# Residual sums two items further on, a row store ahead of other stores, and one load moved into the y products

## Chip, cores and metric

The kernel runs on one core of a Trainium2 chip. The metric is the time of one execution on the device, in microseconds. Engines are named as the profile names them: PE (TensorE), DVE (VectorE), ACT (ScalarE), POOL (GpSimd), SP (SyncE, which issues the DMAs here).

## The reference, cut to what matters

```python
x = A_x                                      # 1 x 2048 x 512, float32
for _ in range(2):                           # two layers
    n = layernorm(x)
    a, b = n @ dft_hid_re.T, n @ dft_hid_im.T
    x = x + (dft_seq_re @ a - dft_seq_im @ b)        # Fourier mixing over the sequence
    n = layernorm(x)
    h = gelu(layernorm(n) @ w1)                      # then shifted by +1, -1, +2, -2 rows
    x1 = n + shifted(h) @ w2
    x = x + x1 + gelu(layernorm(x1) @ w3) @ w4
```

The change touches the Fourier mixing: its residual sum, the sums over rows that the next layernorm needs, and the order of the work beside it.

## The kernel before

All products run in a split form: a float32 operand is cast to a high part (fp32r) and a low part (what is left of it), and each product is three matmuls, high by high, high by low, low by high (`mm3`, line 294). Matrices come through *items*. An item is a block of 128 x 1024 words that is loaded raw by SP (`issue_dma`, line 208), turned into its high part (`stage_one`) and its low part (`stage_two`), and used by TensorE as the moving operand.

- A *plain* item: ScalarE casts the raw block (L241), VectorE subtracts to get the low part (L258).
- A *one* item (half as wide): VectorE first takes a difference of the two halves of a raw block (L243), ScalarE casts it (L244), VectorE makes the low part (L258).
- A *by1* or *by0* item: VectorE takes a difference of two raw blocks (L247), ScalarE casts it (L248), VectorE makes the low part (L258).

Parts lie in a ring of four places. `stream()` hands item i to TensorE; as it does so it issues stage one of item i + 3 (whose place is that of item i - 1, so this waits until TensorE is through with i - 1) and stage two of item i + 2. Each engine takes its instructions in the order in which the program issues them.

The mixing of a layer runs over four chunks (c = 0 to 3) of 512 output rows. A chunk has two phases.

**x products** (`x_phase`): for k = 0 to 7 a plain and a one item, here called x0 to x15; x(2k) feeds PSUM banks PC and PB, twelve matmuls, x(2k+1) feeds PA, six. From chunk 1 on, the eight items of the hidden DFT for the chunk before stand between them (h0 to h7, twelve matmuls each, into PD): h3 in front of x8, h4 and h5 in front of x10, h6 and h7 in front of x12. h0 to h3 give the first half of the chunk's rows, h4 to h7 the second half. When a half is complete, `add_y` adds PD to the residual rows: two SCALAR_TENSOR_TENSOR of VectorE (L596), each with the sum over the row. The first half's rows stand in X0 (tmp rows 0 and 1), the second half's in X1 (tmp rows 4 and 5). After the last x item, ScalarE copies PC, PB (L518, L520) and later PA (L526) to SBUF.

**y products** (`y_phase`): for k = 0 to 7 a by1 item (PC, then PD) and a by0 item (PB, then PA), here called y0 to y15, twelve matmuls each. The first matmul of y0 writes PC again.

Around each x item i stand three things, in this order: `stream()`, `run_late(i)` (small work that was put off to this item) and `hook(i)`. `late[9]` holds the squares of the first half's rows and `late[10]` their statistics; the second half's are done in the y phase. The hook of layer 0 also prepares weights for later stages: sums of weight blocks (`sum_at`: load, make, low part and keep, each at an item's number) and splits of weight blocks (`W_REST`: load, high, low part with its store). In chunks 1 and 2 a third weight sum uses tmp rows 0 to 3 (`sum_t`): its load stands at 11, its three adds (L492) and cast (L1646) at 13, its low part (L1650) at 14, its store at 18. `W_REST` uses tmp rows 2 and 3. Both therefore wait for earlier stores from tmp.

The hook loads the residual rows into X1 at 4 and X0 at 5, and stores X0's finished rows to x1d at 9. In chunk 3 it also brings back rows of x1d (`BACK`): rows 0 and 1 at item 8, 2 and 3 at 11, 4 and 5 at 13 (units of 128 rows). These rows are normed in the stage behind the y products; 4 and 5 during the second of its four hidden products.

All DMAs stand in SP's one queue, and an issue that has to wait for a tile holds up those behind it.

## Time and profile before

| | us |
|---|---|
| median of 3 runs | 1419.0 (1418.55 to 1420.17) |
| the profiled execution | 1418.97 |
| its span, first to last instruction | 1417.2 |
| PE busy | 1409.0 |
| VectorE busy | 1191.3 |
| ScalarE busy | 765.5 |

The granted TensorE clock was 1.000 over the whole span. A timeline row has the start in us, the duration in us, the engine, the line, the operation and the names of what it writes and reads; `x2` means that two neighbours were merged, and a bracket gives the idle time of the engine before it and what ended that. Instructions of one engine overlap at their ends: the distance from start to start is what one costs in a row of several. A row of the view of waits has the total wait in us, how often it occurred, and the longest. An SPq row is the issue of a DMA, not its transfer.

### The profile page before, as it was taken

The page shows a single profiled execution, that of the slowest core. Times are in us where ns is not written, and L with a number is a line of the kernel's source. Part 1 is how long each engine was busy: PE and PEld are TensorE (multiplying, and loading weights), DVE is VectorE, ACT ScalarE, POOL GpSimd, SP SyncE. Part 2 cuts the span into 40 slices and gives each one's busy share as a digit, 9 for nine tenths or more (in the row PEclk, how much of TensorE's full clock was granted, in tenths as well). Part 3 has the DMA queues.
Part 4 walks back from the last instruction along what each step waited for, and adds up shares of the span by engine and source line. Part 5 has one row for each costly group of instructions (what it writes and reads, how often), then busy time and mean ns, then how long its engine had stood idle before and what let it go on. Part 6 is the DMA issues. An engine that isn't in the chain of part 4 may idle for free.

```text
span 1417.2 us, 18479 instructions
## 1 busy us (share of the span) xinstructions
PE 1409.0 (99%) x6669; PEld 1181.8 (83%) x6669; DVE 1191.3 (84%) x1684; ACT 765.5 (54%) x1072; POOL 68.2 (5%) x105
## 2 busy tenths in 40 slices
PE   9999999999999999999999999999999999999998
PEld 8888788888788888988888888888888888899887
DVE  7988998998988789956789979879889788897776
ACT  6664555556566655534555545645555566454351
POOL 2100000000001100000000000000000020000000
PEclk9999999999999999999999999999999999999999
DMA  8978858778774748865556476565587457687864
GB/s 290 306 236 302 268 194 274 241 230 309 255 228 146 253 165 264 257 247 180 195 177 218 136 225 206 166 220 170 193 265 237 134 141 245 188 250 252 297 205 160
DMA packets 158907, 316.18 MB, mean 223 GB/s; under 512 B 10848, under 2 KB 78816, under 8 KB 156896
## 3 DMA queue, kind: packets, MB, share of 16 engines
q1 hardware_dynamic: 158816, 315.01, 67.9%
q8 instruction: 52, 0.85, 0.2%
q14 instruction: 39, 0.32, 0.1%
HBM read 260.70 MB, written 54.26 MB: 222 GB/s over the span
## 4 chain that ended last, share of the span: by engine, by line
PE 94%; DVE 3%; DMA 1%; ACT 1%; issue 1%; SPq 0%; POOL 0%; DVEq 0%; ACTq 0%; POOLq 0%
PE psd L295 10%; PE psd L296 10%; PE psd L297 10%; PE psa L295 8%; PE psa L297 8%; PE psa L296 8%; PE psb L296 7%; PE psb L297 7%; PE psb L295 7%; PE psc L295 6%; PE psc L296 6%; PE psc L297 6%; DMA raw<-in_ws 1%; DVE ring L258 1%; DVE rest L492 0%
## 5 line engine op out<-in xcount | busy, mean ns | idle before, releaser
L241 ACT CAST ring<-raw 128x1024 fp32r<-128x1024 f32 x127 | 132.9, 1052 | 69.4 <-PE psd L297 30.6
L258 DVE TENSOR_TENSOR ring<-raw,ring 128x1024 fp32r<-128x1024 f32 x126 | 153.4, 1220 | 14.3 <-ACT ring L241 14.3
L295 PE MATMUL psd<-ring,rr 128*128 128x512 f32 x208 | 80.9, 389 | 0.0
L296 PE MATMUL psd<-ring,rr 128*128 128x512 f32 x208 | 80.9, 389 | 0.0
L297 PE MATMUL psd<-ring,rr 128*128 128x512 f32 x208 | 80.9, 389 | 0.0
L248 ACT CAST ring<-ring0f 128x1024 fp32r<-128x1024 f32 x28 | 29.5, 1054 | 46.9 <-DVE ring0f L247 46.9
L258 DVE TENSOR_TENSOR ring<-ring1f,ring 128x512 fp32r<-128x512 f32 (+1 forms) x56 | 53.3, 952 | 0.8 <-ACT ring L244 0.7
L346 POOL TENSOR_TENSOR rows<-ve,mhalf 128x4 f32<-128x4 f32 x16 | 18.2, 1136 | 735.2 <-DVE ve L345 735.2
L295 PE MATMUL psc<-ring,ay 128*128 128x512 f32 x128 | 50.0, 391 | 1.6 <-ACT rr11f L518 1.6
L296 PE MATMUL psb<-ring,ay 128*128 128x512 f32 x128 | 50.0, 391 | 1.2 <-DVE ring L258 1.2
L297 PE MATMUL psb<-ring,ay 128*128 128x512 f32 x128 | 49.8, 389 | 0.0
L295 PE MATMUL psb<-ring,ay 128*128 128x512 f32 x128 | 49.8, 389 | 0.0
L296 PE MATMUL psc<-ring,ay 128*128 128x512 f32 x128 | 49.8, 389 | 0.0
L297 PE MATMUL psc<-ring,ay 128*128 128x512 f32 x128 | 49.8, 389 | 0.0
L297 PE MATMUL psa<-ring,ay 128*128 128x512 f32 x126 | 49.0, 389 | 0.0
L295 PE MATMUL psa<-ring,ay 128*128 128x512 f32 x126 | 49.0, 389 | 0.0
L295 PE MATMUL psd<-ring,ay 128*128 128x512 f32 x126 | 49.0, 389 | 0.0
L296 PE MATMUL psd<-ring,ay 128*128 128x512 f32 x126 | 49.0, 389 | 0.0
L296 PE MATMUL psa<-ring,ay 128*128 128x512 f32 x126 | 49.0, 389 | 0.0
L297 PE MATMUL psd<-ring,ay 128*128 128x512 f32 x126 | 49.0, 389 | 0.0
L314 POOL TENSOR_TENSOR rs<-ve,mhalf 128x2 f32<-128x2 f32 (+2 forms) x33 | 28.5, 863 | 412.4 <-DVE nb L313 393.4
L697 DVE TENSOR_TENSOR rg<-gt,rg 128x512 fp32r<-128x512 f32 x32 | 22.1, 690 | 29.6 <-ACT rg L696 29.6
(834 smaller groups left out, 4617.1 us busy)
## 6 DMA issues: line engine op xcount, KB each, us to landing
raw<-in_ws SPq DMA_DIRECT2D x183, 512.0 KB, 5.4
raw<-in_hs SPq DMA_DIRECT2D x56, 512.0 KB, 3.7
w3b<-w3d SPq DMA_DIRECT2D x11, 1792.0 KB, 8.5
w4r<-w4d SPq DMA_DIRECT2D x22, 512.0 KB, 3.5
un<-w4s SPq DMA_DIRECT2D x40, 256.0 KB, 3.7
un<-w4d SPq DMA_DIRECT2D x38, 256.0 KB, 4.4
x1d<-tmp SPq DMA_DIRECT2D x12, 512.0 KB, 6.8
xs<-x1d SPq DMA_DIRECT2D x12, 512.0 KB, 5.2
```

What stands on the lines that cost most here:

```text
L241: nc.scalar.copy(dest[:, a:b, 0], r[0][:, a:b])
L248: nc.scalar.copy(dest[:, :, 0], lo)
L258: nc.vector.tensor_tensor(lo, src, hi.bitcast(F32), op=ALU.subtract)
L295: nc.tensor.matmul(o, lh, rh, start=first, stop=False, skip_group_check=more)
L296: nc.tensor.matmul(o, lh, rl, start=False, stop=False, skip_group_check=more)
L297: nc.tensor.matmul(o, ll, rh, start=False, stop=last, skip_group_check=more)
L314: nc.gpsimd.tensor_tensor(rs[:, :n], ve[:, :n], mhalf[:, 0, :n], op=ALU.pow)
L346: nc.gpsimd.tensor_tensor(rs, ve, mhalf[:, :, :2], op=ALU.pow)
L697: nc.vector.tensor_tensor(lo, src, hi.bitcast(F32), op=ALU.subtract)
```

## The change

Four edits:

1. `add_y` is no longer called right behind the hidden product. The first half's stands in `late[8]` (behind `stream()` of x8), the second half's in `late[13]` (behind `stream()` of x13). This holds for chunks 1 to 3 of both layers. The squares and statistics stay where they were.
2. The third weight sum is made at 12 and its low part at 13, in place of 13 and 14 (chunks 1 and 2 of layer 0).
3. In the hook, the row loads at 4 and 5 and the row store at 9 are issued in front of the weight work of the same item (layer 0).
4. Rows 4 and 5 are brought back at y's k = 5 in place of item 13 (chunk 3 of both layers).

```diff
-BACK = {8: 0, 11: 2, 13: 4}
+BACK = {8: 0, 11: 2}
...
                 if h % 4 == 3:
-                    at_mix = c == NC - 1 and h > 4
-                    add_y(c - 1, h // 4, PD, X1 if h > 4 else X0, 2 * k + 1 if h < 4 else "y", "10" if at_mix else 2 * k + 2 if h < 4 else "y+")
+                    if h < 4:
+                        args = (c - 1, 0, PD, X0, 2 * k + 1, 2 * k + 2)
+                    else:
+                        args = (c - 1, 1, PD, X1, "y", "10" if c == NC - 1 else "y+")
+                    late.setdefault(2 * k + h // 4, []).append(lambda args=args: add_y(*args))
                 h += 1
...
         if c < 3:
-            sum_at(c, *units[2], sum_t, 11, 13, 14, 18)
+            sum_at(c, *units[2], sum_t, 11, 12, 13, 18)
...
-                if layer == 0:
-                    prepare_at(c, i)
-                    for f, n in W_REST.get((c, i), ()):
-                        f(n)
                 j = (c - 1) * TC
                 if i == 4:
                     rows(X1, xin, j + 2, 2, True)
                 if i == 5:
                     rows(X0, xin, j, 2, True)
                 if i == 9:
                     rows(X0, x1d, j, 2, False)
+                if layer == 0:
+                    prepare_at(c, i)
+                    for f, n in W_REST.get((c, i), ()):
+                        f(n)
...
+                if c == NC - 1 and k == 5:
+                    rows(xs[2], x1d, 4, 2, True)
```

## The prediction

> **What bounds the kernel now.** I read the page's busy shares first, then who TensorE waits for, then the timeline of TensorE around each of those waits.

> ```profile
> PE 1409.0 (99%) x6669; PEld 1181.8 (83%) x6669; DVE 1191.3 (84%) x1684; ACT 765.5 (54%) x1072; POOL 68.2 (5%) x105
> ...
> PE psc L295 <- ACT rr11f L518: 1.6, 2, 0.8
> PE psb L296 <- DVE ring L258: 1.2, 1, 1.2
> ...
> 148.16 0.39 PE L297 MATMUL psa<-ring,ax 128*128 128x512 f32 x1
> 149.31 0.50 PE L295 MATMUL psc<-ring,ay 128*128 128x512 f32 x1 [0.76 <-ACT rr11f L518]
> 149.65 0.40 PE L296 MATMUL psc<-ring,ay 128*128 128x512 f32 x1
> ...
> 354.73 0.39 PE L295 MATMUL psb<-ring,ay 128*128 128x512 f32 x1
> 356.27 0.50 PE L296 MATMUL psb<-ring,ay 128*128 128x512 f32 x1 [1.15 <-DVE ring L258]
> ...
> 361.62 0.39 PE L295 MATMUL psb<-ring,ay 128*128 128x512 f32 x1
> 362.07 0.50 PE L296 MATMUL psb<-ring,ay 128*128 128x512 f32 x1
> ```

> TensorE is busy 99% of 1417.2 us, so every microsecond that it waits shows in the time. Matmuls start 0.23 us apart where nothing is late (851.48 to 851.71 in a fence below); a longer step is a stall. Three places matter here. In chunk 1 of layer 0 the first y matmul starts 1.15 after the last x matmul, and the next step is 0.34 instead of 0.23: **1.03** lost. Chunk 2 has its twin (the wait is listed twice): about **1.1**. In chunk 3 the steps at 354.73 and 361.62 are 1.54 and 0.45: 1.31 and 0.22 too long, with 0.11 behind each: **1.76**. So 3.9 us is all that the change could take away.

> **What an x chunk's end hangs on.** VectorE and ScalarE of chunk 1, from the end of the last hidden product (h7) on:

> ```profile
> 139.75 0.69 DVE L596 SCALAR_TENSOR_TENSOR tmp<-psd,tmp 128x512 f32<-128x512 f32 x1 [2.17 <-PE psd L297]
> 140.43 0.69 DVE L596 SCALAR_TENSOR_TENSOR tmp<-psd,tmp 128x512 f32<-128x512 f32 x1
> 141.05 0.69 DVE L243 TENSOR_TENSOR ring3f<-raw 128x512 f32<-128x512 f32 x1
> 141.65 1.22 DVE L258 TENSOR_TENSOR ring<-raw,ring 128x1024 fp32r<-128x1024 f32 x1
> 143.15 1.23 DVE L247 TENSOR_TENSOR ring0f<-raw,raw 128x1024 f32<-128x1024 f32 x1 [0.28 <-PE psb L297]
> 144.29 0.68 DVE L258 TENSOR_TENSOR ring<-ring3f,ring 128x512 fp32r<-128x512 f32 x1
> 144.90 1.60 DVE L492 TENSOR_TENSOR tmp<-tmp 128x512 f32<-128x512 f32 x3
> 146.42 1.22 DVE L247 TENSOR_TENSOR ring1f<-raw,raw 128x1024 f32<-128x1024 f32 x1
> 148.69 1.22 DVE L1650 TENSOR_TENSOR tmp<-tmp 128x1024 fp32r<-128x1024 f32 x1
> ...
> 147.72 1.05 ACT L248 CAST ring<-ring1f 128x1024 fp32r<-128x1024 f32 x1
> 148.68 1.07 ACT L518 COPY rr11f<-psc 128x512 f32<-128x512 f32 x2
> ```

> In order: the two residual sums; x15's difference and x14's low part; y0's difference (ring0) and x15's low part; the three weight sums; y1's difference (ring1); later the weights' low part (L1650). ScalarE casts y1's high part as soon as its difference is there, then empties PC (two copies of 0.53), and the first y matmul writes PC. So **the start of the y products follows y1's difference**: 146.42 + 1.30 to the cast, 0.96 to the copy, 0.58 for its first half, 0.05 to TensorE, 149.31. Whatever stands ahead of y1's difference on VectorE counts in full once this chain is late.

> **The change, part by part.** *Second residual sums, behind x15's low part.* x15's difference writes the ring place of h7, so it can't start before h7 ends (140.41) wherever the sums stand. Before, the first sum ran in that wait for nothing and only the second cost 0.62. After, both stand in a stretch with no idle time ahead of y1's difference: 1.30 (139.75 to 141.05).

> Chunk 1, layer 0, with the weight sums at 12 and their low part at 13, from 140.43: 0.60 (x15's difference, 141.05 to 141.65) + 1.14 (x14's low part; what is 1024 wide steps by 1.14, as 143.15 to 144.29) = 142.17; weight sums 1.52 (144.90 to 146.42) = 143.69, past the 143.13 for which y0's difference waited, so that 0.28 of idle is used; 1.14 + 0.61 = 145.44; residual sums 1.30 = 146.74; the weights' low part, which stood behind y1's difference and now stands ahead of it, 1.14 = 147.88. y1's difference moves from 146.42 to 147.88: **+1.4 to 1.5** on a stall that is already there. (The weight load must be in by 142.17 for this. Here the row store was the last that it waited for, so it goes out sooner and I take it to be in time; it was in by 144.90, so 2.7 more is the utmost.)

> Chunks without weight sums have some slack (chunk 1 of layer 1; its chunks 2 and 3 look the same; then chunk 3 of layer 0):

> ```profile
> 848.22 1.22 DVE L247 TENSOR_TENSOR ring1f<-raw,raw 128x1024 f32<-128x1024 f32 x1
> 849.52 1.05 ACT L248 CAST ring<-ring1f 128x1024 fp32r<-128x1024 f32 x1 [0.68 <-DVE ring1f L247]
> 850.49 1.06 ACT L518 COPY rr11f<-psc 128x512 f32<-128x512 f32 x2
> 851.48 0.39 PE L297 MATMUL psa<-ring,ax 128*128 128x512 f32 x1
> 851.71 0.39 PE L295 MATMUL psc<-ring,ay 128*128 128x512 f32 x1
> ...
> 345.68 1.06 ACT L518 COPY rr11f<-psc 128x512 f32<-128x512 f32 x2
> 346.57 0.39 PE L295 MATMUL psc<-ring,ay 128*128 128x512 f32 x1
> ```

> The first copy ends 850.49 + 0.58 + 0.05 = 851.12; TensorE wants it at 851.71: slack 0.59. Pushed by 1.30 (1.22 where neither sum waits), it is 0.63 to 0.71 late, and the slow step adds 0.11: **+0.8** in each of three chunks, 2.4. In chunk 3 of layer 0 the slack is 346.57 - 346.31 = 0.26: 1.04 + 0.11 = **+1.1**.

> *First residual sums, one item on, and chunk 2's loads.*

> ```profile
> 220.30 0.68 DVE L596 SCALAR_TENSOR_TENSOR tmp<-psd,tmp 128x512 f32<-128x512 f32 x1
> 221.94 1.22 DVE L258 TENSOR_TENSOR ring<-raw,ring 128x1024 fp32r<-128x1024 f32 x1 [0.34 <-ACT ring L241]
> ...
> SPq L1629 <- DMA x1d<-tmp: 2.7, 1, 2.7
> ...
> 228.87 1.35 SPq L1598 DMA_DIRECT2D w3d<-tmp  x2
> 230.26 0.82 SPq L206 DMA_DIRECT2D x1d<-tmp  x1
> ...
> 236.37 0.90 SPq L1629 DMA_DIRECT2D tmp<-in_w  x2
> ...
> DMA to landing us min/median/max: 6.4/6.5/6.6
> ...
> 240.80 1.23 DVE L258 TENSOR_TENSOR ring<-raw,ring 128x1024 fp32r<-128x1024 f32 x1
> ...
> 244.01 1.61 DVE L492 TENSOR_TENSOR tmp<-tmp 128x512 f32<-128x512 f32 x3
> ```

> In chunks 2 and 3 the first sums filled the time until ScalarE's cast of h4 was ready, for which its low part still waited 0.34. Behind that low part they push what follows by 1.2 to 1.3: h5's low part and the load that it frees, the stores behind that, and the loads behind the stores. TensorE itself isn't held: PD's first half is free at 221.94 + 1.14 + 0.69 = 223.8, and h4 needs it two items (eighteen matmuls, 4.08) after h3, which ended about when the first sum started, 220.30: some half us in hand. In chunk 1 and in layer 1 VectorE reached this place before h3 had ended, so the sums cost nothing there. Putting the row store first doesn't free chunk 2's weight load (L1629): it fills all four rows of tmp, and two of them are the source of the w3d stores (L1598), which are now last. The load landed at 236.84 + 6.6 = 243.4; I expect 243.4 to 244.7. The weight sums, one item earlier, want it at 240.80 + 1.14 = 241.94. This is **the new wait**: VectorE stands, with y0's difference, x15's low part (TensorE needs it, and will stall inside x15), the residual sums and y1's difference queued behind. From a landing of 244.3: weight sums 245.85, 1.75 to 247.6, residual sums 248.9, low part 250.0. y1's difference stood at 244.01 + 1.52 = 245.53, so chunk 2 costs **+4.3** (3.6 at 243.4, 4.8 at 244.7; 2.1 if the load is in time).

> [...] The change moves the wait earlier and, in chunk 2, the issue not at all. [...]

> In chunk 3 the weight load at 10 waits for a w3d store that now stands behind the row store, and y0's raw stands behind that load in SP's queue: between nothing and the 1.3 of the shift; I take 0.4.

> *Rows 4 and 5.*

> ```profile
> 344.14 1.43 SPq L206 DMA_DIRECT2D xs<-x1d  x1
> 353.86 1.23 DVE L247 TENSOR_TENSOR ring0f<-raw,raw 128x1024 f32<-128x1024 f32 x1 [1.57 <-DMA raw<-in_ws]
> ...
> xs<-x1d SPq DMA_DIRECT2D x12, 512.0 KB, 5.2
> ```

> In chunk 3 of layer 0 this load holds SP for 1.43 and moves 512 KB ahead of y's raw loads; VectorE then stands 1.57 for one of them, and the low part behind it is what TensorE waits for at 356.27. Gone, and with TensorE itself later by 1.1 or more, both stalls vanish: **-1.76**. At its new place (after ten y items of twelve matmuls, 2.72 each) it has six y items and a hidden product, some 21 us, until ScalarE norms the rows, against 5.2 to land: nothing; without that cover it would cost what of 5.2 is left. Layer 1 has no such stall: nothing. X0's and X1's loads ahead of other loads: they land before the sums that read them, which would wait for them otherwise: nothing.

> **Sum:** 1.4 + 4.3 + (1.1 + 0.4 - 1.76) + 2.4 = +7.8 or +7.9. The profiled run took 1418.97 (span 1417.2), the median is 1419.0: **1427**.

> **Rivals.** (1) *Chunk 2's load is in time*, because the queue empties faster with another order. For it: the issue at 236.37 hangs on stores that could be issued sooner. Against it: the same bytes go ahead. Chunk 2 costs 2.1, and the sum is +5.7: 1424.7. (2) *Faster*: at the end of the x products there is slack that I don't see, so that y1's difference may be 1.3 later for nothing. It decides at y1's cast: with 0.7 more slack layer 1 costs nothing, and if the weights' low part also fits, the three stalls go: -3.9, 1415.1. For it: VectorE idles 2.17 ahead of the old place of the sums. Against it: x15's difference can't use that time, and cast and copy follow without a gap. (3) *No change*: the work moves in TensorE's shadow, and only chunk 1 of layer 0, already late, loses its 1.4, and chunk 3's 1.76 pays for it: 1418.6. [...] The waits listed above speak against it. (4) *Much slower*: the late first sums push chunk 3's raw load as far as chunk 2's weight load, and y0 there costs 4.3 in place of 1.5: 1429.7, or more.

> **Chances.** Forecast 0.53, with its own range 1425.5 to 1429 (the bounds of chunks 2 and 3); rival 1 0.22; rival 2 0.09; rival 3 0.08; rival 4 0.08. The range 1422 to 1430 leaves out rivals 2 and 3 and half of 4. By 0.2%, 2.8 us (about what a measurement of this kernel can tell from no change): faster 0.09, same 0.08, slower 0.83.

> **What would show it.** Right: a wait of TensorE on L518 at all six ends of x products, about 0.7 in layer 1, over 2 in chunk 1 of layer 0 and more in chunk 2; VectorE idle before the weight sums in chunk 2, released by the load; no wait at chunk 3's y0 to y5 for a raw load. Wrong: layer 1's y products follow the x products without a gap, or y1's difference stands ahead of the residual sums.

## The result, and the profile after

| | before | after |
|---|---|---|
| median of 6 runs each, us | 1418.97 (1418.52 to 1420.57) | 1432.09 (1429.86 to 1433.05) |
| ratio after / before | | 1.0087 (1.0074 to 1.0100) |
| the profiled execution | 1418.97 | 1429.93 |
| its span | 1417.2 | 1428.0 |
| granted clock, mean over the span | 1.000 | 0.998 |

The change costs 13.1 us. The forecast was 1427, with a range to 1430: the side was right, the size 5.1 too small. The six runs of the kernel after are not alike: two took 1429.86 and 1429.93 at a mean granted clock of 0.998, four took 1431.94 to 1433.05 at 0.996. Before, the clock was 1.000.

The profile's page and its view of TensorE's waits, kernel after (columns of the second: who waited for what, us in total, times, longest):

```profile
PE 1411.7 (99%) x6669; PEld 1181.6 (83%) x6669; DVE 1190.6 (83%) x1684; ACT 764.5 (54%) x1072; POOL 67.4 (5%) x105
```

```profile
PE psc L295 <- ACT rr11f L521: 8.8, 6, 3.7
PE psa L296 <- DVE ring L258: 1.2, 1, 1.2
PE psb L296 <- DVE ring L258: 0.2, 1, 0.2
```

The copy of PC (L518 before, L521 now) is waited for six times in place of two: at the end of the x products of every chunk that has a residual sum. The wait on `psa` is the stall inside x15 in chunk 2 of layer 0. VectorE is as busy as before (1191.3 and 1190.6), and PE's busy time rose by 2.7 with the same 6669 instructions. Nothing was added; matmuls became slower. Where, the windows of that kernel show (columns: stretch in us and its length, busy us of PE, PEld, DVE, ACT, POOL with counts, **granted clock**, DMA share, GB/s). The stretches are 3.41 long and laid at the edges at which the clock changed:

```profile
148.58:151.99 3.41, 1.79 (x8) 1.49 (x9) 3.41 (x4) 3.37 (x6) 0.00 (x0) 1.00 0.63 195
151.99:155.40 3.41, 3.41 (x17) 2.83 (x16) 3.41 (x4) 2.49 (x4) 0.00 (x0) 1.00 0.61 189
247.56:250.97 3.41, 1.43 (x5) 0.86 (x5) 3.41 (x8) 1.23 (x2) 0.00 (x0) 1.00 0.21 85
250.97:254.38 3.41, 0.81 (x2) 0.72 (x3) 3.41 (x4) 2.39 (x5) 0.00 (x0) 0.50 0.40 117
254.38:257.79 3.41, 3.41 (x9) 2.63 (x9) 3.19 (x3) 3.41 (x6) 0.00 (x0) 0.50 0.66 207
257.79:261.20 3.41, 3.41 (x16) 2.80 (x16) 2.36 (x2) 1.11 (x2) 0.00 (x0) 1.00 0.80 296
```

Around the end of chunk 2's x products the clock is at half for two stretches, each behind one in which TensorE stood idle for long (1.98 and 2.60, which is 3.41 less its busy time; the stall inside x15 counts towards the first). In the second, TensorE is busy all the time and gets 9 matmuls through, in place of 16 or 17. A step there is 0.427, against 0.227 at full clock:

```profile
254.59 0.63 PE L297 MATMUL psc<-ring,ay 128*128 128x512 f32 x1
255.01 0.63 PE L295 MATMUL psc<-ring,ay 128*128 128x512 f32 x1
```

The long wait is thus paid twice, once as a wait and once as slow matmuls behind it. In chunk 1 (the first two rows of the windows) TensorE stood idle for 2.13 and the clock stayed at 1.00. (Two numbers for one stall are kept apart below: *idle* is the time in a timeline's bracket; *late* is what the step from the last matmul to this one has above 0.227, some 0.16 more. What a place *loses* is late, plus the 0.11 of the step behind it, plus slow matmuls.)

VectorE in chunk 2, kernel after:

```profile
241.05 1.23 DVE L258 TENSOR_TENSOR ring<-raw,ring 128x1024 fp32r<-128x1024 f32 x1
245.06 1.61 DVE L492 TENSOR_TENSOR tmp<-tmp 128x512 f32<-128x512 f32 x3 [2.79 <-DMA tmp<-in_w]
246.59 1.22 DVE L247 TENSOR_TENSOR ring0f<-raw,raw 128x1024 f32<-128x1024 f32 x1
247.72 0.69 DVE L258 TENSOR_TENSOR ring<-ring3f,ring 128x512 fp32r<-128x512 f32 x1
...
250.68 1.22 DVE L247 TENSOR_TENSOR ring1f<-raw,raw 128x1024 f32<-128x1024 f32 x1
```

This is the new wait, as forecast: VectorE stands 2.79 for the load of the weight rows; x15's low part comes at 247.72, too late for TensorE; y1's difference comes at 250.68, when TensorE had been through with x15 since 249.9; before, it came at 245.53, ahead of the last x matmul (247.21). And the end of an x phase of layer 1, TensorE:

```profile
859.38 0.39 PE L297 MATMUL psa<-ring,ax 128*128 128x512 f32 x1
860.23 0.50 PE L295 MATMUL psc<-ring,ay 128*128 128x512 f32 x1 [0.46 <-ACT rr11f L521]
860.57 0.39 PE L296 MATMUL psc<-ring,ay 128*128 128x512 f32 x1
```

A step of 0.85 and one of 0.34 where 0.23 each would do: 0.73, three times.

### The profile page after: what moved, and what is told of

Read it like the earlier page. It is cut to its first block, busy times and chain, and to the rows that moved or that the text cites. A ratio compares the mean times of both kernels' runs of the same rounds, so it can differ in the third digit from the quotient of the medians.

```text
span 1428.0 us, 18485 instructions
## 1 busy us (share of the span) xinstructions
PE 1411.7 (99%) x6669; PEld 1181.6 (83%) x6669; DVE 1190.6 (83%) x1684; ACT 764.5 (54%) x1072; POOL 67.4 (5%) x105
## 4 chain that ended last, share of the span: by engine, by line
PE 90%; DVE 5%; DMA 2%; ACT 2%; issue 1%; SPq 0%; DVEq 0%; POOL 0%; ACTq 0%
PE psd L295 9%; PE psd L296 9%; PE psd L297 9%; PE psa L295 8%; PE psa L297 8%; PE psa L296 8%; PE psc L295 6%; PE psb L296 6%; PE psb L295 6%; PE psb L297 6%; PE psc L296 6%; PE psc L297 6%; DVE ring L258 1%; DMA tmp<-in_w 1%; DVE ring0f L247 1%
## 5 line engine op out<-in xcount | busy, mean ns | idle before, releaser
L241 ACT CAST ring<-raw 128x1024 fp32r<-128x1024 f32 x127 | 132.6, 1051 | 68.6 <-PE psd L297 29.2
L258 DVE TENSOR_TENSOR ring<-raw,ring 128x1024 fp32r<-128x1024 f32 x126 | 153.6, 1220 | 18.5 <-ACT ring L241 18.2
L297 PE MATMUL psd<-ring,rr 128*128 128x512 f32 x208 | 80.9, 389 | 0.0
L296 PE MATMUL psd<-ring,rr 128*128 128x512 f32 x208 | 80.9, 389 | 0.0
L295 PE MATMUL psd<-ring,rr 128*128 128x512 f32 x208 | 80.9, 389 | 0.0
L295 PE MATMUL psc<-ring,ay 128*128 128x512 f32 x128 | 51.0, 399 | 8.8 <-ACT rr11f L521 8.8
L248 ACT CAST ring<-ring0f 128x1024 fp32r<-128x1024 f32 x28 | 29.5, 1054 | 46.3 <-DVE ring0f L247 46.0
L258 DVE TENSOR_TENSOR ring<-ring1f,ring 128x512 fp32r<-128x512 f32 (+1 forms) x56 | 53.3, 951 | 0.8 <-ACT ring L244 0.7
L248 ACT CAST ring<-ring1f 128x1024 fp32r<-128x1024 f32 x28 | 29.5, 1053 | 43.5 <-DVE ring1f L247 43.5
L296 PE MATMUL psc<-ring,ay 128*128 128x512 f32 x128 | 50.3, 393 | 0.0
L297 PE MATMUL psc<-ring,ay 128*128 128x512 f32 x128 | 50.3, 393 | 0.0
L296 PE MATMUL psb<-ring,ay 128*128 128x512 f32 x128 | 50.0, 391 | 0.2 <-DVE ring L258 0.2
L297 PE MATMUL psb<-ring,ay 128*128 128x512 f32 x128 | 49.8, 389 | 0.0
L295 PE MATMUL psb<-ring,ay 128*128 128x512 f32 x128 | 49.8, 389 | 0.0
L295 PE MATMUL psd<-ring,ay 128*128 128x512 f32 x126 | 49.4, 392 | 0.0
L297 PE MATMUL psd<-ring,ay 128*128 128x512 f32 x126 | 49.3, 391 | 0.0
L296 PE MATMUL psd<-ring,ay 128*128 128x512 f32 x126 | 49.3, 391 | 0.0
L297 PE MATMUL psa<-ring,ay 128*128 128x512 f32 x126 | 49.0, 389 | 0.0
L296 PE MATMUL psa<-ring,ay 128*128 128x512 f32 x126 | 49.0, 389 | 0.0
L295 PE MATMUL psa<-ring,ay 128*128 128x512 f32 x126 | 49.0, 389 | 0.0
## 6 DMA issues: line engine op xcount, KB each, us to landing
raw<-in_ws SPq DMA_DIRECT2D x183, 512.0 KB, 5.3
raw<-in_hs SPq DMA_DIRECT2D x56, 512.0 KB, 3.9
w4r<-w4d SPq DMA_DIRECT2D x22, 512.0 KB, 3.8
x1d<-tmp SPq DMA_DIRECT2D x12, 512.0 KB, 6.8
xs<-x1d SPq DMA_DIRECT2D x12, 512.0 KB, 5.7
```

What stands on the lines that cost most here:

```text
L241: nc.scalar.copy(dest[:, a:b, 0], r[0][:, a:b])
L248: nc.scalar.copy(dest[:, :, 0], lo)
L258: nc.vector.tensor_tensor(lo, src, hi.bitcast(F32), op=ALU.subtract)
L295: nc.tensor.matmul(o, lh, rh, start=first, stop=False, skip_group_check=more)
L296: nc.tensor.matmul(o, lh, rl, start=False, stop=False, skip_group_check=more)
L297: nc.tensor.matmul(o, ll, rh, start=False, stop=last, skip_group_check=more)
```

## The experiments

**Theory:** nearly everything that the change costs comes from what stands ahead of y1's difference on VectorE, and what the waits themselves don't explain comes from the granted clock, which falls behind a long wait. **Rivals:** the extra time has nothing to do with the wait's length (the moved stores and loads compete with others); or the queue is not it, and the loads alone set the x phases' ends. In all of them the instructions of one kernel keep their names, but line numbers move by a few.

| run | from | edit | median, us (low to high) | ratio to before (interval) |
|---|---|---|---|---|
| e1 | after | weight sums back to 13 and 14 | 1427.47 (1426.52 to 1428.97) | 1.0053 (1.0038 to 1.0068) |
| e2 | after | second sums at once | 1424.44 (1424.16 to 1425.94) | 1.0035 (1.0023 to 1.0048) |
| e4 | before | second sums alone put off | 1427.50 (1425.26 to 1428.36) | 1.0050 (1.0035 to 1.0065) |
| e5 | before | idle subtractions in layer 1 | 1432.54 (1431.45 to 1433.17) | 1.0087 (1.0072 to 1.0102) |
| e6 | after | first sums at once | 1430.40 (1427.89 to 1430.84) | 1.0070 (1.0056 to 1.0084) |
| e7 | after | row loads and store back | 1428.85 (1428.08 to 1430.50) | 1.0064 (1.0048 to 1.0079) |
| e3 | before | rows 4, 5 in the y products | 1418.71 (1417.78 to 1420.39) | 0.9995 (0.9986 to 1.0003) |
| e8 | before | e3, and weight sums at 14 and 17 | 1422.11 (1420.81 to 1424.64) | 1.0015 (1.0007 to 1.0024) |
| r1, r2 | after | none | 1431.41; 1433.13 | one run each |
| e10 | after | second sums at 14, weight sums at 18, 20 | 1417.40 (1416.33 to 1418.34) | 0.9986 (0.9977 to 0.9995) |
| e12 | before | e3, and weight sums at 18, 20 | 1416.76 (1415.33 to 1417.73) | 0.9979 (0.9970 to 0.9988) |

The kernel before had 1419.24 (beside e1, e2, e4, e5), 1419.29 (e3, e6, e7, e8) and 1419.46 (the rest).

### e1: the weight sums where they were

```diff
-            sum_at(c, *units[2], sum_t, 11, 12, 13, 18)
+            sum_at(c, *units[2], sum_t, 11, 13, 14, 18)
```

> The changed kernel with the third weight sum back at 13 and its low part at 14. Queue theory: the wait for chunk 2's weight load goes, since the sums stand behind the residual sums again (which end near 245.2, the load lands near 244.9). y1's difference then starts about 1.3 later than before the change in chunks 1 and 2, so the stalls there are about 2.3 us each; chunk 3 and layer 1 stay as in the changed kernel (+0.9, +2.2). Clock theory (the granted clock falls because TensorE waited 3.7 us in chunk 2): no wait above 2.5 us is left, the granted clock is 1.000 in every run, the time 1424 to 1425. Rival (the clock falls by itself, whatever TensorE waits): the clock stays at 0.996 to 0.998 and the time is 1426 to 1428.

Measured: chunk 2's stall inside x15 is gone, and y0 is 2.24 late in place of 3.85. That part of the forecast holds: the 2.79 for the load came from the earlier place. But the clock isn't 1.000. The windows of e1 in chunk 1:

```profile
148.11:151.52 3.41, 1.43 (x7) 0.88 (x6) 3.41 (x4) 3.27 (x6) 0.00 (x0) 1.00 0.41 131
151.52:154.93 3.41, 3.41 (x10) 2.63 (x9) 3.41 (x4) 2.74 (x6) 0.00 (x0) 0.50 0.48 179
```

An idle time of 1.98 was followed by a half-clock stretch in chunk 1, and chunk 2 shows the same; the chunks lost 3.85 and 3.95, of which 1.60 in each are slow matmuls. In the profile of the kernel after, 2.13 in chunk 1, which is longer, cost no clock. So the length of the wait alone doesn't decide; r1 and r2 below show what else does.

### e2, e6: one residual sum put back

```diff
-                    late.setdefault(2 * k + h // 4, []).append(lambda args=args: add_y(*args))
+                    if h < 4:
+                        late.setdefault(2 * k, []).append(lambda args=args: add_y(*args))
+                    else:
+                        add_y(*args)
```

> The changed kernel with the second half's residual sums back behind h7; the first half's stay late. Queue theory: the three waits of 0.6 us at the ends of layer 1's x products are gone (-2.2), chunk 1 of layer 0 stalls about 1.7 in place of 2.4, and chunk 2 still waits for its weight load inside x15 (1.3) and then some 2.6 in place of 3.85 at y0. Clock theory: the wait of 2.6 is too short to bring the clock down, or does so in some runs only; time 1424 to 1425 without, 2 to 3 more with it. Rival (the position of the second sums doesn't matter, the loads do): layer 1's waits stay and the time is 1430.

e6 is the mirror image (first sums at once, second put off):

> The changed kernel with the first half's residual sums back behind h3. Queue theory: VectorE no longer falls 1.3 us behind in chunks 2 and 3 of layer 0, the stores and loads behind h5's low part go out about 1.3 earlier, chunk 2's weight load lands near 243.6 in place of 244.9, and TensorE loses some 4 us there in place of 5.3 before the clock; chunk 3's y0 loses 1.1 in place of 1.9. Without the clock +6; with one to three half-clock windows of 3.4 us (each up to 1.7) 1426.5 to 1429.5. Rival (the store order alone makes the load late): chunk 2 stays as in the changed kernel, time 1431 to 1432.

The waits of TensorE in e2:

```profile
PE psc L295 <- ACT rr11f L524: 4.3, 3, 2.5
PE psa L296 <- DVE ring L258: 1.1, 1, 1.1
```

Three waits in place of six: with the second sums ahead of x15's difference again, layer 1 waits nowhere. This is the largest single part, and it is VectorE's queue and nothing else that was touched. One half-clock stretch is left, in chunk 2, where y0 is 2.63 late. In e6 VectorE stands 1.02 for chunk 2's weight rows in place of 2.79, so the put-off first sums had made that load later; there is no stall inside x15, y0 is 3.40 late in place of 3.85, and chunk 2 loses 5.12 in place of 7.37. In chunk 3 VectorE no longer waits for y0's raw load:

```profile
349.00 1.23 DVE L247 TENSOR_TENSOR ring0f<-raw,raw 128x1024 f32<-128x1024 f32 x1 [0.89 <-PE psb L297]
```

There y0 loses 1.07 in place of 1.89. Layer 1 keeps its three times 0.73. But in chunk 1 VectorE now stands 0.58 ahead of the weight sums (the trace names no releaser), y0 is 2.96 late, and the clock falls: 4.67 in place of 2.40. One place gives back most of what the others gained, so the median, 1430.40, lies above the expected 1429.5.

### e4: the second sums alone

```diff
+                    if h < 4:
+                        add_y(c - 1, 0, PD, X0, 2 * k + 1, 2 * k + 2)
+                    else:
+                        args = (c - 1, 1, PD, X1, "y", "10" if c == NC - 1 else "y+")
+                        late.setdefault(2 * k + 1, []).append(lambda args=args: add_y(*args))
```

> The kernel before with one edit: the second half's residual sums at item 13. Queue theory: layer 1 gets a wait of 0.62 us at each of three ends of x products (+2.2), chunks 1 and 2 of layer 0 get 1.2 to 1.3 more each, chunk 3 gets 1.1 and loses part of its 1.76 behind it since TensorE is later: 1424 to 1425.5, clock 1.000. Rival (VectorE's idle time ahead of the old place covers the sums): the time stays at 1419.

Five lines of the change, with every store, load and weight sum as before, cost 8.3 us. In the profile: chunk 1 loses 3.85 in place of 1.03, chunk 2 3.85 in place of 1.10, y0 of chunk 3 1.06, where it lost nothing, layer 1 three times 0.73. The expected 1424 to 1425.5 had the waits, but not the clock: it was to stay at 1.000. In chunk 1 TensorE was idle for 1.98 of one stretch (147.57 to 150.98, busy for 1.43 of 3.41), and the next was at half clock; chunk 2 lost as much, and the mean clock, 0.998, fits one such stretch in each. No transfer was moved here, so competition between transfers isn't needed for the clock's fall.

### e5: waits made on purpose

Two, three and four subtractions of 128 x 1024 on VectorE, ahead of y1's difference in chunks 1, 2 and 3 of layer 1, where the kernel before has no wait at all. They write rows of `tmp` that nobody reads after that.

```diff
+                if layer and i == 13:
+                    for _ in range({1: 2, 2: 3, 3: 4}[c]):
+                        nc.vector.tensor_tensor(tmp[:, 2:4], tmp[:, 2:4], tmp[:, 2:4], op=ALU.subtract)
```

> The kernel before with 2, 3 and 4 idle subtractions of 128x1024 on VectorE (1.14 us each) ahead of y1's difference in chunks 1, 2 and 3 of layer 1; they write a scratch tile, nothing of the result. Queue theory: TensorE waits 1.7, 2.8 and 4.0 us at the three y0, 8.5 us in all with the slow first steps 8.8: 1427.8 at a clock of 1.000. Clock theory: the wait of 4.0 halves the clock for 3.4 to 7 us behind it, the wait of 1.7 never, the wait of 2.8 rarely or not: 2 to 4 us on top, clock 0.996 to 0.998. Rival (the clock falls by itself or for the loads): clock 1.000 and matmul steps of 0.23 behind all three waits.

The windows of e5, at the edges of its clock, one pair for each chunk:

```profile
850.79:854.20 3.41, 1.78 (x9) 1.16 (x7) 3.41 (x4) 1.67 (x3) 0.00 (x0) 1.00 0.15 50
854.20:857.62 3.42, 3.42 (x15) 2.83 (x16) 3.42 (x4) 3.42 (x7) 0.00 (x0) 1.00 0.72 259
953.18:956.59 3.41, 1.37 (x6) 1.16 (x7) 3.41 (x4) 2.96 (x6) 0.00 (x0) 1.00 0.49 161
956.59:960.01 3.42, 3.42 (x10) 2.68 (x9) 3.04 (x4) 2.90 (x5) 0.00 (x0) 0.50 0.64 206
1055.58:1058.99 3.41, 0.00 (x0) 0.00 (x0) 3.41 (x4) 1.35 (x2) 0.00 (x0) 1.00 0.12 30
1058.99:1062.41 3.42, 3.19 (x8) 2.54 (x9) 3.42 (x4) 3.42 (x8) 0.00 (x0) 0.50 0.77 277
```

The y products are 1.79, 3.05 and 4.31 late: 1.26 more for each further subtraction, so what stands ahead of y1's difference counts in full. The chunks lose 1.90, 4.76 and 5.87. Less that and the 0.11 of the step behind it, that leaves 0, 1.60 and 1.45. A first row with TensorE idle for 1.63 (3.41 less 1.78) is followed by full clock; idle for 2.04 or 3.41, by half clock. (The expectation had the first and the last right; the middle wait was taken to be mostly harmless.) Nothing of the change is in this kernel. **The clock's fall follows here from waiting alone** (0.50 behind idle times of 2.04 and 3.41).

### r1, r2: the kernel after, looked at again

> The changed kernel once more, unaltered, for a second profile. Clock theory: the granted clock is set per window of 3.41 us, the windows run on from the kernel's start, and a window in which TensorE idles 1.98 us or more is followed by one at half clock, one with 1.64 or less is not. Chunk 1's wait (2.1 us) falls into one window or is split over two, by where the windows happen to lie, so some executions lose 1.6 us there and others nothing; chunk 2 always drops. Where the time is 1432 or more, chunk 1 shows matmul steps of 0.43 behind its wait; where it is 1430, it doesn't. Rival (the slower executions wait longer for loads): TensorE's waits differ in length and the clock record doesn't.

> The same kernel a third time, with the same expectation: chunk 1 at half clock behind its wait if and only if one window holds at least 1.98 us of its idle time.

The windows of r1 in chunk 3, then those of r2 in chunk 1:

```profile
353.81:357.22 3.41, 1.39 (x7) 1.14 (x7) 3.41 (x4) 2.94 (x6) 0.00 (x0) 1.00 0.90 286
357.22:360.63 3.41, 3.41 (x10) 2.67 (x9) 3.41 (x5) 3.41 (x6) 0.00 (x0) 0.50 0.91 306
```

```profile
148.20:151.61 3.41, 1.49 (x6) 1.24 (x7) 3.41 (x4) 3.07 (x6) 0.00 (x0) 1.00 0.54 166
151.61:155.02 3.41, 3.41 (x9) 2.67 (x8) 3.12 (x4) 2.79 (x4) 0.00 (x0) 0.50 0.65 192
```

Each has the two half-clock stretches of chunk 2 and a third one: r1 behind an idle time of 2.02 in chunk 3, r2 behind the 2.12 of chunk 1. The third cost 1.60 in r1 and 1.59 in r2. Chunk 1's idle time is the same in all three profiles (2.13, 2.13, 2.12); what differs is where the stretches of 3.41 lie, which are thus not laid from the span's start. They run on between the changes of the clock: e1's at 151.52 and 253.92 and e5's at 956.59 and 1058.99 are both 102.40 apart, 30.0 stretches. Counted back so from 250.97 in the first profile, an edge at 148.58 splits chunk 1's idle time into 0.5 and 1.62; from 357.22 in r1, one at 149.00 splits it into 0.9 and 1.2; in r2 1.92 (3.41 less 1.49) of it falls between 148.20 and 151.61, less than the 1.98 that was expected to be needed. In chunk 1, then, the place of the wait decides.

r1 was expected to show its third stretch in chunk 1, and shows it in chunk 3. There the wait itself was longer, 2.02 in place of 1.62, because VectorE stood longer for y0's raw load (1.39, in place of 0.85):

```profile
349.67 1.23 DVE L247 TENSOR_TENSOR ring0f<-raw,raw 128x1024 f32<-128x1024 f32 x1 [1.39 <-DMA raw<-in_ws]
```

So the rival, longer waits for loads, holds for a part of it: here they lifted the wait from 1.62, which full clock followed, to 2.02, which half clock followed. The mean clock of the six runs fits two kinds: two stretches at half clock take 2 x 3.41 x 0.5 / 1428 = 0.0024 off it, three 0.0036; two of the six runs show 0.998, the four others 0.996. That those four had a third stretch is worked out from their mean clock alone; no profile of them shows it.

### e7: row loads and row store back behind the weight work

The block `if layer == 0: prepare_at ... W_REST` stands in front of the three `rows` again; all else is as after.

> The changed kernel with loads and row store back behind the weight work of the same item. If the same bytes ahead of the load set its landing, chunk 2's load lands as late as in the changed kernel (within 0.5 us), and chunk 1's weight load lands later than there, so that the weight sums of chunk 1 wait for it: 1431 to 1434. Rival (putting the row store first made chunk 2's load late): chunk 2's wait inside x15 shrinks below 0.5 us, 1427 to 1429.

TensorE's waits in chunk 2 of e7, from its timeline:

```profile
247.89 0.50 PE L296 MATMUL psa<-ring,ax 128*128 128x512 f32 x1 [0.51 <-DVE ring L258]
253.00 0.80 PE L295 MATMUL psc<-ring,ay 128*128 128x512 f32 x1 [3.69 <-ACT rr11f L521]
```

The stall inside x15 is 0.51, against 1.18, 0.91 and 1.02 in the three profiles of the kernel after, so the row store in front did delay that load, as the rival has it. But chunk 2 as a whole loses 7.46 in place of 7.37: more matmuls fell into its half-clock stretches. Chunk 1 has the same idle time as after (2.13), so its weight sums don't wait for their load; the theory said that they would. In chunk 3 the stall at y3 is gone and 0.09 of that at y5 is left (0.73 for both in the first profile of the kernel after). That can't be put down to the edit: in r2, which is the kernel after once more, TensorE stands idle for 1.14 at y3. The first profile, then r2:

```profile
364.22 0.50 PE L296 MATMUL psb<-ring,ay 128*128 128x512 f32 x1 [0.16 <-DVE ring L258]
```

```profile
367.44 0.50 PE L296 MATMUL psb<-ring,ay 128*128 128x512 f32 x1 [1.14 <-DVE ring L258]
```

The medians of e7 and of the kernel after differ by 3.2; what makes that up was not followed.

### e3: rows 4 and 5 alone

```diff
-BACK = {8: 0, 11: 2, 13: 4}
+BACK = {8: 0, 11: 2}
...
+                if c == NC - 1 and k == 5:
+                    rows(xs[2], x1d, 4, 2, True)
```

> The kernel before with one edit: rows 4 and 5 loaded at y's k = 5. Theory: the stalls at y3 and y5 of chunk 3 in layer 0 (1.76 us) go and nothing else changes: 1417.2, clock 1.000. Rival (the raw loads were late for another reason): the stalls stay, 1419.

No difference in the time that can be measured. The stall at y3 falls from 1.43 to 0.66, the one at y5 stays (0.34 and 0.33). VectorE and TensorE of e3 in chunk 3:

```profile
346.35 1.23 DVE L247 TENSOR_TENSOR ring2f<-raw,raw 128x1024 f32<-128x1024 f32 x1 [0.67 <-DMA raw<-in_ws]
...
355.43 0.50 PE L296 MATMUL psb<-ring,ay 128*128 128x512 f32 x1 [0.39 <-DVE ring L258]
```

Without the load of the rows, VectorE still stands 0.67 for a raw load of the y items. The load of the rows is thus not the only reason for the late raw loads. These two profiles differ by 0.78 there, but that is no price for the edit: with the code of before in that place, e5 has an idle time of 1.43 at y3 (before 1.15), and with e3's edit e12 has 1.22 (e3 0.39).

### e8, e10, e12: a better place for the sums

If all that counts is what stands ahead of y1's difference, the weight sums should go behind it. e8 puts them to 14 and 17 in the kernel before, with e3's edit:

```diff
-            sum_at(c, *units[2], sum_t, 11, 13, 14, 18)
+            sum_at(c, *units[2], sum_t, 11, 14, 17, 18)
```

> The kernel before with rows 4 and 5 loaded at y's k = 5 and the third weight sum later in place of earlier: its adds at 14, behind y1's difference, its low part at 17. Queue theory: nothing stands ahead of y1's difference any more, the stalls of chunks 1 and 2 (1.03 and 1.10) go as well as chunk 3's 1.76: 1415.1 to 1415.5, clock 1.000. Rival (the weight sums only move the stall to y1 or y2): 1417 or more.

The expectation was missed by some 7 us: chunks 1 and 2 lose 2.1 each, twice what they lost before. ScalarE at the end of chunk 1's x products, e8 first, then the kernel before:

```profile
145.85 1.06 ACT L248 CAST ring<-ring1f 128x1024 fp32r<-128x1024 f32 x1 [0.68 <-DVE ring1f L247]
148.46 1.04 ACT L1646 CAST tmp<-tmp 128x1024 fp32r<-128x1024 f32 x1 [1.54 <-DVE tmp L492]
149.41 1.07 ACT L518 COPY rr11f<-psc 128x512 f32<-128x512 f32 x2
```

```profile
146.53 1.05 ACT L1646 CAST tmp<-tmp 128x1024 fp32r<-128x1024 f32 x1 [1.01 <-DVE tmp L492]
147.72 1.05 ACT L248 CAST ring<-ring1f 128x1024 fp32r<-128x1024 f32 x1
```

VectorE did make y1's difference 1.5 earlier (1.75 behind y0's, where it was 3.27), but the cast of the weight sums (L1646) goes to ScalarE at the same item, and at 14 it stands ahead of the copies of PC. ScalarE idles 1.54 for the adds before it may copy. The work left one queue's critical place and took another's.

e10 moves the weight sums on to 18, 20 and 21, inside the y products, and the second residual sums to 14, behind y1's difference, in the kernel after. e12 is e3 with the weight sums at 18, 20 and 21 and the residual sums as before:

```diff
-            sum_at(c, *units[2], sum_t, 11, 12, 13, 18)
+            sum_at(c, *units[2], sum_t, 11, 18, 20, 21)
...
-                    late.setdefault(2 * k + h // 4, []).append(lambda args=args: add_y(*args))
+                    late.setdefault(2 * k + 2 * (h // 4), []).append(lambda args=args: add_y(*args))
```

> The changed kernel with the second residual sums at 14 in place of 13 (behind y1's difference, in front of y2's) and the third weight sum in the y products: adds at 18, low part at 20, store at 21. Queue theory: nothing new stands ahead of y1's difference on VectorE nor ahead of the copies of PC on ScalarE, so the waits at the ends of layer 1's x products and of chunks 1 and 2 go; chunk 3 keeps its late raw loads (0.5 to 1.9). Clock 1.000, 1416.5 to 1418.5. Rival (the late first sums and the store order alone make y0 late): chunk 2 keeps over 2 us and the time is 1421 or more.

> The kernel before with rows 4 and 5 loaded at y's k = 5 and the third weight sum in the y products: adds at 18, low part at 20, store at 21, so that neither the adds on VectorE nor the cast on ScalarE stand ahead of y1's cast and the copies of PC. Queue theory: the stalls of chunks 1 and 2 go (-1.03, -1.10) and chunk 3 has the 0.78 less that the rows alone gave: 1416.3, clock 1.000. Rival (the sum only moves the stall, as at 14): a wait of 1 us or more in y4 to y8 of chunks 1 and 2, 1418 or more.

VectorE in chunk 1 of e10, and then ScalarE and TensorE there in e12:

```profile
143.79 0.69 DVE L258 TENSOR_TENSOR ring<-ring3f,ring 128x512 fp32r<-128x512 f32 x1
144.39 1.22 DVE L247 TENSOR_TENSOR ring1f<-raw,raw 128x1024 f32<-128x1024 f32 x1
145.53 1.22 DVE L258 TENSOR_TENSOR ring<-ring0f,ring 128x1024 fp32r<-128x1024 f32 x1
146.66 0.69 DVE L599 SCALAR_TENSOR_TENSOR tmp<-psd,tmp 128x512 f32<-128x512 f32 x1
```

```profile
145.90 1.05 ACT L248 CAST ring<-ring1f 128x1024 fp32r<-128x1024 f32 x1 [0.69 <-DVE ring1f L247]
146.86 1.06 ACT L518 COPY rr11f<-psc 128x512 f32<-128x512 f32 x2
```

```profile
147.86 0.39 PE L297 MATMUL psa<-ring,ax 128*128 128x512 f32 x1
148.09 0.39 PE L295 MATMUL psc<-ring,ay 128*128 128x512 f32 x1
```

The y products follow the x products at 0.23, without a gap. In e10 the same residual sums, one item further on than in the change, cost nothing at the ends of the x products but 0.27 in chunk 3 of layer 0. No stall cost any clock in either. e12 has the lowest median, 2.7 us under the kernel before; its stalls of chunks 1 and 2 are gone as expected, but chunk 3 keeps its 1.22 at y3. e10's interval overlaps with e12's, so which of the two places of the residual sums is better isn't settled.

## Why the prediction was right on the side and wrong in size

Losses of TensorE at each place, profiled execution of after less that of before, beside the prediction's terms:

| place | predicted | waits | slow matmuls |
|---|---|---|---|
| chunk 1, layer 0 | +1.4 | +1.37 (2.40 less 1.03) | 0 |
| chunk 2 | +4.3 | +4.31 (x15 1.45 and y0 3.96, less 1.10) | +1.96 |
| chunk 3 | -0.26 (1.1 + 0.4 - 1.76) | +0.86 (y0 1.89, y3 and y5 0.73, less 1.76) | 0 |
| layer 1 | +2.4 | +2.18 (3 x 0.73) | 0 |
| sum | +7.9 | +8.7 | +2.0 |

The waits and the slow matmuls sum to 10.7; the spans differ by 10.8.

- **Right: the queue.** Chunk 1, chunk 2 and layer 1 came within some 0.2 of their terms, by the path that was named: sums ahead of y1's difference, cast, copy of PC, first y matmul. e2 took the second sums out and layer 1's waits went; e5 put other work in and they came, 1.26 for each subtraction.
- **Right: chunk 2's new wait.** The load was expected between 243.4 and 244.7. VectorE went on at 245.06, with TensorE 0.8 further on in time than before (x15's first matmul at 246.89 and 246.08): 244.3 in the forecast's count. Rival 1 (the load in time) is out. That the term came out to 0.01 is luck: the prediction's own steps lead from 244.3 to 250.0, which is 4.5 behind 245.53 and not 4.3. Chunk 2 was the worst of the six (7.37 lost in the profile of the kernel after), and e1, which waits one item later, has no wait for this load.
- **Wrong in size: chunk 3.** "Both stalls vanish: -1.76" was too much: 0.73 of the stalls is left in the first profile of the kernel after, and 1.75 in r2. How much the edit is worth is not settled (e3, e7). And y0's raw load cost more than the 0.4 that was taken; the sign that the prediction named, no wait for a raw load there, didn't come:

```profile
349.19 1.23 DVE L247 TENSOR_TENSOR ring0f<-raw,raw 128x1024 f32<-128x1024 f32 x1 [0.85 <-DMA raw<-in_ws]
```

## What to carry to other kernels

Price a wait of TensorE by what it does to its clock as well: where chunk 1's stall grew from an idle time of 0.76 (before) to 2.13 (after), it cost what it grew by (1.37), and 1.6 on top in r2 but not in the first profile. Before moving small work "further on", find the one instruction in its queue that releases the bottleneck next, and put the work behind it: one item too early cost 8.3 us (e4), one item later, in a kernel that also had the weight sums out of the way, next to nothing (e10 beside e12). Then follow the work's other halves too, the cast on ScalarE and the load on SP, past the critical instructions of their own queues (e8, and chunk 2).

## What the runs showed of the hardware

- **The granted clock and idle time.** With stretches of 3.41 counted from the clock's edges, the full-clock stretches that half clock followed had TensorE idle for 1.92 (r2), 1.98 (the kernel after, e1, e2 and e4), 2.02 (r1), 2.05 (e6), and 2.04 and 3.41 (e5). Full clock followed idle times of 1.62 (the kernel after), 1.63 (e5) and 1.67 (around the last matmuls of the kernel after), and every shorter one in the profiles of before and after. An idle time between 1.67 and 1.92 was not seen in these stretches. A stretch that was already at half clock was followed by another one when idle for 2.60 (the kernel after) and 0.94 (r2: from 254.01 to the matmul at 254.95), and by full clock when idle for 0.58 (e2: busy for 2.84 of 3.42).
- **The step behind a wait.** In the profiles of before and after, the second matmul behind each of the ten waits of TensorE with full clock on both sides, idle for 0.16 to 2.13, starts 0.335 to 0.341 behind the first, in place of 0.227: 0.11 for each of them. Behind the one that ends at half clock (253.57) it is 0.59, in place of 0.427.
